# Fourier stage of a two-layer FNet and multi-query kernel: y tiles as 64-row matmuls in the score banks, a block's layer norm by VectorE, query weights split two steps ahead, and other times for the early maxima

## The chip, the cores and the metric

The kernel runs on one core of one Trainium2 chip. The metric is device time in microseconds (us), the median of repeated runs. The engines are named as in the profile: PE is TensorE's matmul (PEld its weight load), DVE is VectorE, ACT is ScalarE, POOL is GpSimd, SP is SyncE, which issues most DMAs. Each engine runs its own queue in program order. The kernel writes that order out by hand: the schedule is manual, and an instruction stands on its engine's queue where the code called it.

## The reference, cut to what matters

Two layers, each a Fourier mixing (A) and a multi-query attention (B), on 2048 rows of 512 numbers, all in float32:

```python
def _A_ref(x, dft_seq_re, dft_seq_im, dft_hid_re, dft_hid_im):
    a = jnp.einsum("bsd,ed->bse", x, dft_hid_re)
    b = jnp.einsum("bsd,ed->bse", x, dft_hid_im)
    return jnp.einsum("ts,bse->bte", dft_seq_re, a) - jnp.einsum("ts,bse->bte", dft_seq_im, b)

def _B_ref(x, wq, wk, wv, wo):            # 32 query heads of 16, one key and value head
    q = (x @ wq) ...; k = x @ wk; v = x @ wv
    p = _softmax(einsum(q, k) * 16 ** -0.5)
    return (p @ v) ... @ wo

x = A_x
for _ in range(2):
    x = x + _A_ref(_layernorm(x), ...)
    x = x + _B_ref(_layernorm(x), ...)
```

## The kernel before

A float32 product is made of three fp32r matmuls: both factors are split into a high part (a cast) and a low part (what is left), and `mm3` adds high by high, high by low, low by high. So every product below is three matmuls per 128 rows of contraction, and each operand needs a split: a cast on ACT, a subtraction on DVE or POOL.

Phase A of a layer (`phase_a`) makes the Fourier mixing, the keys and values, the queries, and some of the row maxima that the softmax needs. The 2048 output rows go in four blocks, `tb` 0 to 3, of 512. A block has 32 z steps: step `n` of phase A (0 to 127) belongs to block `n // 32`, to the cosine (c = 0) or sine (c = 1) half, and to one of 16 tiles of 128 input rows. In a step the matrix tile `craw` (loaded by SP six steps ahead, `c_load`, and split two steps ahead by ACT and POOL, `c_split`) is multiplied with the normalised input `xnh`, `xnl`: twelve matmuls of 128 rows by 512 columns. The sum over 16 steps, z, stands in four PSUM banks, two tiles of two banks named `x` (`pair()`, of which there are two; in phase B they hold the scores). After 16 steps `evac` splits z into `zh`, `zl`.

After a block's 32 steps, `y_tile` makes the block's four output tiles: 24 matmuls each of z with the hidden matrix (`dh`, `dl`), in a bank named `y` (three of them), then DVE adds the residual, POOL stores the tile, DVE takes the layer norm's sums (`ln_stats`). Block 3 is made apart, in the tail.

Then, among the first twelve z steps of the next block, run the block's tasks (`prep_tasks`, called "prep" below): the inverse deviation (`ln_rstd`), the layer norm (`ln_apply`), transposes (`tr`, into the one bank `z`), keys and values (`kv`, `v_tr`), and for four groups of heads the split of the query weights (`wq_load`, `wq_split`), the queries (`q_mm`) and their store to DRAM (`q_store`). Tasks stand in a dictionary by step, and run behind that step's matmuls.

`z_rows` makes two steps at a time with matmuls of 64 rows of contraction instead of 128: the upper and the lower 64 rows write two different banks, and in a second phase (`ph`) the other two. Between the two phases ACT copies two numbers of the bank to `junk`, which orders the writes of the two halves into one bank. `by_rows(n)` says from which step on: before, n >= 48, that is from the second half of block 1.

The maxima: for a query tile `i`, a key block `kb` and a pair of heads, `max_pair` makes two matmuls of 64 rows (one per row half) into two `y` banks, and DVE reduces each to its row maximum. Most are made in phase B, beside the scores, but 16 entries `(i, kb)` of the table `EARLY`, of 16 head pairs each, are made in phase A. An entry is (i, kb, slot of its queries, step of their load, start, end): its 16 pairs are spread evenly from start to end, on a scale in which a block takes 40 units, 32 for its z steps and 8 for its y tiles (each of the 32 groups of three matmuls of a block's y is a quarter of a unit). `hook` puts them into `inner`, and `within` calls them between the matmuls.

## Time and profile before

| | |
|---|---|
| median of 3 runs | 3801.16 us (3798.8 to 3802.88) |
| the profiled execution, its own time | 3804.91 us |
| its span, first to last instruction | 3803.1 us |
| busy: PE, PEld | 3675.1 us (97%), 1903.4 us (50%) |
| busy: DVE, ACT, POOL | 2793.1 us (73%), 2389.6 us (63%), 826.6 us (22%) |
| mean granted TensorE clock | 0.987 |
| phase A of the two layers, from its first matmul to the first scores | about 10 to 730 us, and 1905 to 2620 us |

Busy times of PE are those of pipelined matmuls, whose recorded spans overlap, so a busy PE still may issue slowly; the distance from one start to the next tells more. A merged row of the timeline that ends in "x2" holds two instructions. The clock column of a stretch is the mean share of full speed that was granted. A wait is put down to the work that ended last before it.

### The profile page before, as it was taken

How to read it: one execution, taken by the hardware profiler on the slowest of the kernel's cores; microseconds unless marked ns; L12 is line 12 of the kernel's file. 1: busy time of each engine (PE TensorE's matmuls, PEld its weight loads, DVE VectorE, ACT ScalarE, POOL GpSimd, SP SyncE). 2: the span in 40 equal slices, each digit the busy share in tenths (PEclk: the TensorE clock that was granted, in tenths of full speed). 3: DMA queues.
4: the chain of work that ended last, by engine and by line, in shares of the span. 5: the costliest groups of instructions: out<-in, count | busy, mean ns of one | idle time of the engine just before them, and what ended most of it. 6: DMA issues, size and time to landing. Idle time of an engine off the chain costs nothing. (4 is left out here: it accounts for less than half of the span.)

```text
span 3803.1 us, 61730 instructions
## 1 busy us (share of the span) xinstructions
PE 3675.1 (97%) x24130; PEld 1903.4 (50%) x24130; DVE 2793.1 (73%) x4743; ACT 2389.6 (63%) x3028; POOL 826.6 (22%) x1008
## 2 busy tenths in 40 slices
PE   8998989999999999999999989899999999999999
PEld 6776657633333333333377666575334333333433
DVE  5175867688888888888311758686888888888882
ACT  3222212488888888888933222225888888888888
POOL 5634333111111111111155342331000000000000
PEclk9999999999999999999999999899999999999999
DMA  5533323311111100110144332233111111001100
GB/s 181 128 131 88 110 72 102 102 32 33 49 35 32 46 21 24 33 49 23 38 133 116 112 100 84 86 92 98 32 46 35 33 33 49 23 22 46 35 22 26
DMA packets 204726, 242.84 MB, mean 64 GB/s; under 512 B 36880, under 2 KB 160784, under 8 KB 197264
## 3 DMA queue, kind: packets, MB, share of 16 engines
q1 hardware_dynamic: 199504, 222.08, 19.6%
q0 software_dynamic: 4864, 16.78, 1.6%
q8 instruction: 189, 3.10, 0.3%
q14 instruction: 105, 0.86, 0.1%
q10 hardware_dynamic: 64, 0.02, 0.0%
HBM read 174.58 MB, written 63.17 MB: 63 GB/s over the span
## 5 line engine op out<-in xcount | busy, mean ns | idle before, releaser
L745 ACT ACTIVATE slot<-x 128x1024 f32<-128x1024 f32 x1990 | 1943.1, 1027 | 334.4 <-PE x L742 271.4
L351 DVE TENSOR_REDUCE mxp<-y 128x1 f32<-128x512 f32 x3040 | 1908.3, 684 | 280.7 <-PE y L350 238.2
L756 PE MATMUL z<-slot,v 128*32 128x512 f32 x8192 | 1096.2, 605 | 1.9 <-ACT row L759 1.9
L742 PE MATMUL x<-slot,kz 64*128 64x512 f32 x2956 | 900.6, 447 | 3.7 <-DMA slot<-mt 3.6
L742 PEld LDWEIGHTS x<-slot,kz 64*128 64x128 f32 x2956 | 375.0, 185 | 731.7 <-ACT slot L745 598.5
L350 PE MATMUL y<-kz,slot 64*128 64x512 f32 x2208 | 726.2, 436 | 4.5 <-ACT mt L381 0.7
L338 DVE TENSOR_REDUCE mxe<-y 128x1 f32<-128x512 f32 x832 | 517.4, 683 | 163.3 <-PE y L336 146.7
L629 PE MATMUL x<-ch,xnh 64*128 64x512 f32 (+1 forms) x1536 | 429.4, 383 | 7.4 <-DVE slot L74 5.6
L796 POOL TENSOR_TENSOR row<-row,row 128x256 f32<-128x256 f32 x63 | 46.2, 733 | 1681.8 <-DMA row<-rd 1179.7
L629 PE MATMUL x<-ch,xnl 64*128 64x512 f32 (+1 forms) x1536 | 399.0, 359 | 0.0
L629 PE MATMUL x<-cl,xnh 64*128 64x512 f32 (+1 forms) x1536 | 398.7, 359 | 0.0
L350 PEld LDWEIGHTS y<-kz,slot 64*128 64x128 f32 x2208 | 349.6, 185 | 94.1 <-DVE mxp L351 27.4
L336 PE MATMUL y<-kz,slot 64*128 64x512 f32 (+1 forms) x1088 | 376.7, 431 | 17.5 <-DVE mxe L338 6.4
L78 POOL TENSOR_TENSOR cl<-craw,ch 128x512 fp32r<-128x512 f32 x236 | 304.8, 1306 | 260.1 <-ACT ch L77 191.7
L756 PEld LDWEIGHTS z<-slot,v 128*32 128x32 f32 x8192 | 163.5, 108 | 277.4 <-issue 249.2
L633 ACT COPY junk<-x 128x2 f32<-128x2 f32 x192 | 30.6, 159 | 390.0 <-PE x L629 296.1
L77 ACT CAST ch<-craw 128x512 fp32r<-128x512 f32 x256 | 154.5, 619 | 172.9 <-PE x L88 75.3
L629 PEld LDWEIGHTS x<-cl,xnh 64*128 64x128 f32 x1536 | 252.1, 190 | 20.5
L629 PEld LDWEIGHTS x<-ch,xnl 64*128 64x128 f32 x1536 | 251.1, 189 | 22.0
L629 PEld LDWEIGHTS x<-ch,xnh 64*128 64x128 f32 x1536 | 236.5, 189 | 35.8 <-issue 11.5
L336 PEld LDWEIGHTS y<-kz,slot 64*128 64x128 f32 x1088 | 180.8, 187 | 146.8 <-DVE mxe L338 90.2
L86 PE MATMUL y<-slot,slot 128*128 128x512 f32 x480 | 208.0, 433 | 17.4 <-ACT slot L77 7.7
(143 smaller groups left out, 3668.7 us busy)
## 6 DMA issues: line engine op xcount, KB each, us to landing
craw<-ct_in SPq DMA_DIRECT2D x112, 512.0 KB
slot<-qd SPq DMA_DIRECT2D x44, 1024.0 KB
qd<-row SPq DMA_DIRECT2D x144, 128.0 KB
od<-row SPq DMA_DIRECT2D x252, 64.0 KB
row<-x_in SPq DMA_DIRECT2D x32, 256.0 KB
mid<-row POOLq DMA_DIRECT2D x32, 256.0 KB, 2.3
craw<-ct_in SPq DMA_DIRECT2D x32, 256.0 KB
row<-mid SPq DMA_DIRECT2D x32, 256.0 KB
```

The lines of the kernel that those rows point to most:

```text
L77: nc.scalar.copy(hi, raw)
L78: (eng or nc.vector).tensor_sub(lo, raw, f(hi))
L86: nc.tensor.matmul(ps_, ah, bh, start=start, stop=False)
L336: nc.tensor.matmul(pm[g], o.qT[i][gs, pr, :], kz[gs, c0:c0 + n], start=True, stop=True)
L338: nc.vector.reduce_max(to[:, g:g + 1], pm[g], axis=AX.X)
L350: nc.tensor.matmul(pm, o.qT[i][gs, pr, :], kz[gs, kb * 512:kb * 512 + 512], start=True, stop=True)
L351: nc.vector.reduce_max(partial(i)[:, pr, g, kb:kb + 1], pm, axis=AX.X)
L629: nc.tensor.matmul(z[d][:, cols], w, hl[j][t == 1][rs_], start=m == 0 and ph == 0 and j == t == 0, stop=j == 1 and t == 2 and (ph == 0 or ...
L742: nc.tensor.matmul(st["e"][:, g, :], kz[64 * g:64 * g + KR, c * P:(c + 1) * P], o.qT[i][64 * g:64 * g + KR, cp:cp + 4, :], start=True, sto ...
L745: nc.scalar.activation(ptiles[i, s_][:, 2 * w:2 * w + 2, :], st.pop("e"), AF.Exp, scale=DH ** -0.5)
L756: nc.tensor.matmul(a[32 * j:32 * j + 32, :], v1[:, c, :], pt[:, j, :], start=c == 0, stop=c == NT - 1)
L796: nc.gpsimd.tensor_mul(bt["ot"][:, cs], bt["ot"][:, cs], bt["den"][:, cs])
```

## The change

It has five parts.

1. `y_rows` makes the y of blocks 0 to 2 (block 3 keeps `y_tile`): all four output tiles at once, as 64-row matmuls in two `pair()` tiles, the banks of z. The first phase adds, for each row half, its half of the contraction to one of the two tiles of a pair, the second phase swaps them, with the `junk` copy of ACT between. The two tiles of the first pair are added, stored and summed after 84 of the 96 pairs of matmuls, those of the second pair at the end. `within` is called after every third pair of matmuls.
2. `by_rows` holds from step 16 on, no longer from 48 on.
3. In prep, DVE applies the layer norm (`apply`), two tiles a step, where POOL applied one a step.
4. The tasks of prep are spread otherwise. In `z_rows` the tasks of the even step run in the middle of the pair of steps (`mid_tasks`), ahead of the second `junk` copy, where they ran at its end. The weights of query groups 0 and 1 are loaded at prep step 2 (before: all at step 4) and split at step 5, those of groups 2 and 3 loaded at step 4 and split right behind `q_mm(0)` and `q_mm(1)`, two steps ahead of their use (before: one). `kv` goes from step 5 to 6, `v_tr` from 6 to 7; `q_store` stands ahead of the next `q_mm`, no longer behind it.
5. `EARLY` has other times for the same 16 entries, and two of them change places.

```diff
 EARLY = [
-    (2, 0, 2, 44, 56, 63), (3, 0, 3, 45, 63, 70), (0, 0, 8, 47, 70, 78), (1, 0, 9, 50, 78, 86),
+    (2, 0, 2, 44, 55, 63), (3, 0, 3, 45, 63, 71), (0, 0, 8, 47, 71, 79.5), (1, 0, 9, 50, 79.5, 88),
...
+        def y_rows(tb, zh, zl, x1, between):
+            yp = [pair(), pair()]
+            at = 0
+            for ph in range(2):
+                for cc in range(2):
+                    for a in range(2):
+                        for kk, k in enumerate((0, 2, 1, 3)):
+                            for t in range(3):
+                                for r in range(2):
+                                    j = (r + ph) % 2
+                                    rs_ = slice(64 * r, 64 * r + 64)
+                                    ts_ = slice((2 * a + j) * P, (2 * a + j + 1) * P)
+                                    w = (zl if t == 2 else zh)[cc][rs_, k, ts_]
+                                    nc.tensor.matmul(yp[a][:, j, :], w, (dl if t == 1 else dh)[cc][rs_, k, :],
+                                                     start=ph == cc == kk == t == 0, stop=cc == 1 and kk == 3 and t == 2,
+                                                     skip_group_check=True)
+                            between(at)
+                            at += 1
+                        if cc == 1 and ph == 0:
+                            nc.scalar.copy(junk, yp[a][:, :, 0])
+                        elif cc == 1:
+                            for j in range(2):
+                                nc.vector.tensor_add(x1[2 * a + j], yp[a][:, j, :], x1[2 * a + j])
+                                nc.gpsimd.dma_start(mid[4 * tb + 2 * a + j], x1[2 * a + j])
+                            for j in range(2):
+                                ln_stats(x1[2 * a + j], 4 * tb + 2 * a + j)
...
-            ts[0] = [alloc, lambda: ln_apply(x1[0], x1[0], 4 * tb, nc.gpsimd)]
-            for j in range(1, 4):
-                ts[j] = [lambda j=j: ln_apply(x1[j], x1[j], 4 * tb + j, nc.gpsimd), lambda j=j: tr(j - 1)]
-            ts[4] = [lambda: tr(3)]
-            ts[4] += [lambda: [wq_load(g) for g in range(4)]]
-            ts[5] = [do_kv, lambda: wq_split(0)]
-            ts[6] = [lambda: v_tr(4 * tb, 4, st["vt"])]
+            def apply(*tts):
+                for tt in tts:
+                    ln_apply(x1[tt], x1[tt], 4 * tb + tt)
+
+            ts[0] = [alloc, lambda: apply(0, 1)]
+            ts[1] = [lambda: apply(2, 3), lambda: tr(0)]
+            ts[2] = [lambda: tr(1), lambda: wq_load(0), lambda: wq_load(1)]
+            ts[3] = [lambda: tr(2)]
+            ts[4] = [lambda: tr(3), lambda: wq_load(2), lambda: wq_load(3)]
+            ts[5] = [lambda: wq_split(0), lambda: wq_split(1)]
+            ts[6] = [do_kv]
+            ts[7] = [lambda: v_tr(4 * tb, 4, st["vt"])]
+            ts[8] = []
             for g in range(4):
-                ts[7 + g] = [lambda g=g: q_mm(tb, g, *st["xt"])]
-                if g:
-                    ts[7 + g].append(lambda g=g: q_store(tb, g - 1))
-                if g < 3:
-                    ts[7 + g].append(lambda g=g: wq_split(g + 1))
-            ts[11] = [lambda: q_store(tb, 3)]
+                ts[7 + g].append(lambda g=g: q_mm(tb, g, *st["xt"]))
+                if g < 2:
+                    ts[7 + g].append(lambda g=g: wq_split(g + 2))
+                ts[8 + g] = [lambda g=g: q_store(tb, g)]
...
             def by_rows(n):
-                return n >= 48
+                return n >= 16
...
-            def z_rows(n, ops, m, cols, c):
+            def z_rows(n, ops, m, cols, c, mid_tasks=lambda: None):
...
                             within((n, 4 * ph + 2 * dd + j))
+                            if ph == 0 and dd == j == 1:
+                                mid_tasks()
                         if ph == 0:
                             nc.scalar.copy(junk, zp[dd][:, :, cols.start])
...
-                    z_rows(n - 1, [(s - 1, hl), (s, hl)], s // 2, slice(0, 512), c)
-                    for fn in tasks.pop(n - 1, ()):
-                        fn()
+                    z_rows(n - 1, [(s - 1, hl), (s, hl)], s // 2, slice(0, 512), c,
+                           lambda: [fn() for fn in tasks.pop(n - 1, ())])
...
                 if n % 32 == 31 and tb < 3:
-                    for tt in range(4):
-                        y_tile(tb, tt, zh, zl, x1[tt], {k: inner.pop(("y", tb, 8 * tt + k), ()) for k in range(8)})
+                    y_rows(tb, zh, zl, x1, lambda k: within(("y", tb, k)))
```

What moves, at three places. On PE, in the y of block 1 of the first layer (`slot_278` to `slot_281` are the hidden matrix, the other slots z's parts and, beside `kz`, the queries; L86 to L88 are `mm3`, L336 a pair of maxima); before:

```order
L86 MATMUL y<-slot_278,slot_1592 128x512
L87 MATMUL y<-slot_279,slot_1592 128x512
L88 MATMUL y<-slot_278,slot_1593 128x512
L336 MATMUL y<-kz,slot_1618 128x512 x2
L86 MATMUL y<-slot_278,slot_1592 128x512
L87 MATMUL y<-slot_279,slot_1592 128x512
L88 MATMUL y<-slot_278,slot_1593 128x512
```

Now (L401 is `y_rows`; "x2" are the two row halves, and the maxima's two are row halves too):

```order
L401 MATMUL x<-slot_278,slot_2067 128x512 x2
L336 MATMUL y<-kz,slot_2143 128x512 x2
L401 MATMUL x<-slot_278,slot_2066 128x512 x2
L401 MATMUL x<-slot_279,slot_2066 128x512 x2
L401 MATMUL x<-slot_278,slot_2067 128x512 x2
```

Before, a pair of 64-row maxima stood between matmuls of 128 rows; now all in this stretch have 64 rows.

On DVE, at the end of the same y and the first steps of prep (`row` are the output tiles, L338 the maxima's reduction); before, the last tile's add and sums, and all that follows up to the maxima in the fourth prep step:

```order
L398 TENSOR_TENSOR row_2075<-y,row_2075 128x512
L135 BN_STATS bst<-row_2075 128x6
L136 BN_AGGR mv<-bst 128x2
L338 TENSOR_REDUCE mxe<-y 128x1 x8
L157 TENSOR_SCALAR lnv<-mv 128x4
L161 RECIPROCAL rs<-lnw 128x4
L173 TENSOR_TENSOR lnw<-rs 128x4
L174 TENSOR_TENSOR lnw<-lnw,lnv 128x4
L176 TENSOR_SCALAR lnw<-lnw 128x4
L178 TENSOR_TENSOR rs<-rs,lnw 128x4
L338 TENSOR_REDUCE mxe<-y 128x1 x16
```

Now, from the second pair's adds on:

```order
L410 TENSOR_TENSOR row_2579<-x,row_2579 128x512
L410 TENSOR_TENSOR row_2581<-x,row_2581 128x512
L135 BN_STATS bst<-row_2579 128x6
L136 BN_AGGR mv<-bst 128x2
L135 BN_STATS bst<-row_2581 128x6
L136 BN_AGGR mv<-bst 128x2
L338 TENSOR_REDUCE mxe<-y 128x1 x4
L157 TENSOR_SCALAR lnv<-mv 128x4
L161 RECIPROCAL rs<-lnw 128x4
```

The adds and sums of two tiles now stand in one lump (the first pair's lump stands two reductions ahead of these rows), the reductions between it and `lnv` are four, not eight, and behind `rs` follow `row_2575<-row_2575,mv,rs` and three more of L182, which POOL had.

On ACT, in the first pair of prep steps of block 1, now (L666 is `junk` of `z_rows`, L159 the square root of `ln_rstd`, L81 and L82 the split behind a transpose):

```order
L666 COPY junk<-x 128x2
L159 ACTIVATE lnw<-lnv 128x4
L666 COPY junk<-x 128x2
L81 ACTIVATE row_5319<-z 128x512
L82 CAST slot_5276<-row_5319 128x4x128
```

Before (L633 is `junk`, L159 the square root):

```order
L633 COPY junk<-x 128x2 x2
L159 ACTIVATE lnw<-lnv 128x4
L81 ACTIVATE row_4687<-z 128x512
L82 CAST slot_4681<-row_4687 128x4x128
L77 CAST ch<-craw 128x512 x2
```

Both copies of `junk` stood ahead of the square root; now it stands between them.

6 rows, old and new, of the table EARLY are left out of this document.

## The prediction

> **What bounds the kernel now.** I read the page first, then the stretches of phase A in the view by windows, then the timeline where a stretch takes longer than its matmuls.
>
> ```profile
> span 3803.1 us, 61730 instructions
> PE 33%; DVE 1%; ACT 0%; DMA 0%; issue 0%; SPq 0%; ACTq 0%; DVEq 0%
> ```
>
> The chain that ended last runs through PE wherever it names an engine. So time is won where PE's starts lie further apart than they must. The change touches phase A alone; phase B keeps the same maxima to make, since `EARLY` holds the same 16 entries. The stretches below are, in order: y of block 0, prep of block 0, steps 46 to 63, y of block 1, its prep (steps 64 to 75), steps 76 to 95, y of block 2, its prep (96 to 107), 108 to 117, 118 to 127, and steps 48 to 129 of the first and of the second layer.
>
> ```profile
> core 0: us, PE busy (x) PEld busy (x) DVE busy (x) ACT busy (x) POOL busy (x), PEclk, DMA share, GB/s
> 107.78:129.89 22.11, 22.09 (x97) 17.94 (x96) 4.71 (x9) 4.13 (x8) 6.83 (x7) 1.00 0.10 36
> 129.89:189.07 59.18, 51.45 (x225) 39.57 (x224) 5.00 (x11) 19.83 (x36) 43.66 (x40) 1.00 0.62 133
> 194.65:257.47 62.82, 60.53 (x482) 47.27 (x480) 46.44 (x74) 17.74 (x42) 25.12 (x21) 1.00 0.50 177
> 257.47:291.59 34.12, 34.12 (x130) 20.26 (x130) 24.68 (x42) 4.31 (x8) 6.57 (x7) 1.00 0.15 54
> 291.59:374.25 82.66, 70.75 (x433) 50.64 (x432) 43.17 (x74) 19.16 (x44) 38.00 (x28) 0.90 0.29 77
> 374.25:453.55 79.30, 77.95 (x599) 54.30 (x599) 72.71 (x119) 21.98 (x52) 30.64 (x24) 1.00 0.43 137
> 453.55:497.84 44.29, 42.02 (x143) 22.69 (x144) 33.56 (x55) 3.48 (x6) 5.55 (x7) 1.00 0.16 61
> 497.84:588.28 90.44, 77.39 (x451) 50.73 (x447) 53.87 (x93) 19.06 (x44) 37.93 (x28) 0.91 0.27 72
> 588.28:634.81 46.53, 44.46 (x453) 35.64 (x454) 41.42 (x69) 13.07 (x35) 17.92 (x14) 0.96 0.41 131
> 634.81:700.61 65.80, 63.25 (x655) 55.39 (x651) 41.21 (x81) 13.91 (x45) 17.48 (x23) 1.00 0.14 47
> 201.61:710.13 508.52, 472.88 (x3369) 340.33 (x3370) 360.66 (x612) 114.68 (x282) 179.56 (x152) 0.96 0.30 94
> 2092.10:2600.98 508.88, 473.20 (x3369) 340.02 (x3369) 360.69 (x612) 114.70 (x282) 179.52 (x152) 0.96 0.30 92
> ```
>
> The first row gives PE's unit: 96 matmuls of 128 by 512 in 22.11 us, 0.23 us each. The two layers' stretches are alike (508.5 and 508.9 us), so I work one layer and double.
>
> What maxima cost between matmuls of 128 rows, and what 64-row pairs cost among themselves:
>
> ```profile
> 258.04 0.40 PE L88 MATMUL y<-slot,slot 128*128 128x512 f32 x1
> 258.36 0.49 PE L336 MATMUL y<-kz,slot 64*128 64x512 f32 x2
> 258.79 0.50 PE L86 MATMUL y<-slot,slot 128*128 128x512 f32 x1
> 259.12 0.39 PE L87 MATMUL y<-slot,slot 128*128 128x512 f32 x1
> ...
> 296.24 0.61 PE L629 MATMUL x<-cl,xnh 64*128 64x512 f32 x2
> 296.47 0.61 PE L629 MATMUL x<-ch,xnl 64*128 64x512 f32 x2
> ```
>
> From L88 to L87 three steps take 1.08 us where three units are 0.69: a round trip from 128 rows to 64 and back costs 0.39 us. Two 64-row matmuls on different halves share one unit (296.24 to 296.47).
>
> The Trainium skill speaks against cutting a matmul in two: "TensorEngine Tiling (Array Packing)", section "Instruction Overhead", gives each matmul about 60 cycles of overhead on this chip. The change issues 1344 more (576 in six y, 768 in the z of steps 16 to 47); at the 2.4 GHz of "TensorE: Matmul & The Clock Gate" that would by estimate be 34 us. The rows above show none of it, since the pair takes 0.23 us as the single does, so the sum goes without it.
>
> Then the waits of prep:
>
> ```profile
> 299.07 0.16 DVE L157 TENSOR_SCALAR lnv<-mv 128x4 f32<-128x4 f32 x1
> 300.31 0.16 DVE L178 TENSOR_TENSOR rs<-rs,lnw 128x4 f32<-128x4 f32 x1
> 300.58 4.13 POOL L182 TENSOR_SCALAR row<-row,mv,rs 128x512 f32<-128x512 f32 x2 [4.48 <-DVE rs L178]
> 302.70 1.12 PE L251 MATMUL z<-ident,row 128*128 128x128 f32 x4 [3.99 <-POOL row L182]
> 306.05 0.63 PE L629 MATMUL x<-cl,xnh 64*128 64x512 f32 x2
> 306.47 0.63 PE L629 MATMUL x<-ch,xnl 64*128 64x512 f32 x2
> ...
> 323.07 0.49 PE L86 MATMUL y<-slot,wkvh 128*128 128x512 f32 x1 [1.40 <-ACT slot L82]
> ...
> 325.45 0.63 PE L87 MATMUL y<-slot,wkvh 128*128 128x512 f32 x1
> 325.87 0.63 PE L88 MATMUL y<-slot,wkvl 128*128 128x512 f32 x1
> ...
> PE z L251 <- POOL row L182: 24.8, 10, 4.8
> PE y L88 <- POOL slot L78: 10.0, 10, 1.4
> PE y L86 <- ACT slot L77: 7.7, 4, 1.9
> ```
>
> PE stood 3.99 us for the layer norm, and then issued at 0.42 us instead of 0.23; it did so again at 325, behind a wait of 1.40. The clock column says why: 0.90 and 0.91 in the two preps is (1 - 0.90) x 2 x 82.66 = 16.5 us at half clock in the first and 16.3 in the second, each worth up to 8 us. The last two rows are the query weights, split too late.
>
> The Trainium skill ("TensorE: Matmul & The Clock Gate", section "What's actually happening") lets the clock fall only after an idle window of about 3.4 us. By that rule all the half-clock time goes once no wait is so long; that is the second case below.
>
> **The sum.** Prices of DVE and ACT:
>
> ```profile
> 440.48 3.68 DVE L338 TENSOR_REDUCE mxe<-y 128x1 f32<-128x512 f32 x6 [0.24 <-PE x L629]
> 463.97 0.68 DVE L398 TENSOR_TENSOR row<-y,row 128x512 f32<-128x512 f32 x1
> 465.51 2.54 DVE L338 TENSOR_REDUCE mxe<-y 128x1 f32<-128x512 f32 x4
> L182 DVE TENSOR_SCALAR row<-row,mv,rs 128x512 f32<-128x512 f32 x24 | 21.4, 894 | 4.5 <-POOL rs L151 4.3
> 355.08 0.60 ACT L81 ACTIVATE row<-y 128x512 f32<-128x512 f32 x1 [7.39 <-PE y L88]
> 355.71 0.62 ACT L82 CAST row<-row 128x512 fp32r<-128x512 f32 x1
> 356.24 0.61 ACT L77 CAST slot<-row 128x512 fp32r<-128x512 f32 x1
> ```
>
> A pair of maxima costs DVE 3.68 / 3 = 1.23 us, a tile's add and sums 1.54 (463.97 to 465.51), the inverse deviation 1.4 (299.07 to 300.47), a tile's layer norm 0.89.
>
> *y of block 1.* Before, 112 units are 25.8 us, 16 round trips 6.2, 2 remain for banks. After, 96 + 15 units are 25.5. New: y takes the banks of z and waits for `evac`. ACT frees the first pair after a copy, a cast, a copy (1.82 us), of which 1.4 (six units) pass beside z. With its handing on 0.7, and 0.5 for reductions that come late. 26.7 for 34.1: -7.4.
>
> *Prep of block 1.* Units: 144 of z, 31 of maxima, 64 of tasks, 239, 55.0 us. Seven stays at 128 rows instead of five cost 2.7. The tasks in mid-pair put ACT work ahead of the second `junk`, for which PE waits; five of them (two transposes, `kv`, two `q_mm`) put 1.2 to 1.9 us there where PE has 1.4 us of matmuls left: 0.5 each, 0.9 for the one with a weights' cast behind it, 2.9. The layer norm: from the first lump on DVE has 3.1 + 1.2 + 3.1 + 2.5 = 9.9 us ahead of `lnv`, then root and `junk` 0.7, and PE gets there after 2.8 + 2.8 + 1.4 + 0.9 = 7.9: it waits 2.7, and 1.8 more for score maxima's banks behind four applications of 0.89. That lump moves the wait more than it removes it. `kv` and the weights have two or three steps and are hidden by z. Of the half clock I keep half, 4 us, since the row at 325 ran slow behind a wait of only 1.40 us; and 0.8 for issue. 69.9 for 82.7: -12.8.
>
> *y of block 2.* Before: 119 units are 27.4, 23 round trips 9.0, and DVE idled a quarter of it. After, PE needs 28 us, DVE 23 x 1.23 + 2 x 1.54 = 31.4 (the second pair's lump comes later); with a wait at the start and at the first lump I take 35: -9.3.
>
> *Prep of block 2.* In its first six steps DVE sets the pace: 21 x 1.23 + 3.1 + 1.4 + 3.6 = 33.9 us against 25 of PE. In the last six, 155 units are 35.7, with three stays 1.2, ACT 2.0, and a second of waiting. Half of the half clock, 4: 77.8 for 90.4: -12.6.
>
> *Steps 76 to 95.* 59 pairs of maxima become 52. Before, DVE was the bound (59 x 1.23 + 1.4 = 74 of 79.3; 1.4 are two subtractions of `evac`, priced like the add's 0.68). After, DVE needs 65.4 and PE 292 x 0.23 = 67.2 and one hand-over of banks, 0.60 + 0.62 and the handing on, 68.6; so near each other I add 3.4: 72.0, -7.3.
>
> *The rest.* 108 to 117 lose three pairs, -3.7. 118 to 127 get nine more: between 9 x 0.23 = 2.1 and 9 x 1.23 = 11.1, I take +6, since DVE is busy 41 of 66 us but not at the same steps. 46 to 63: two units fewer, -0.5. Block 0 has no maxima, so its prep now pays stays at 128 rows (2.7) and ACT (2.9), and loses its waits of 11.3 (59.18 less 208 units): with 1.3 for the lump and 0.7 at y's start, 55.5, and I take -3. Steps 16 to 47 as 64-row pairs: `z_rows` ran 4.8 us over its units in 194.65 to 257.47, with two hand-overs in it; over sixteen pairs between 0 and 8, nearest the clean rows at 0.23: +1.5.
>
> Queues passed: SP now takes two weight loads two steps earlier, where they wait for the transposes of the rows that they overwrite, at most a step; the matrix tiles behind them are wanted four steps on, which covers it. Gone, that cover would cost each block one z step, 2.8 us. POOL loses four times 2.07 us a block and gets nothing. Six stores a group go ahead of a `q_mm` and wait for POOL's subtraction of the step before, as they did.
>
> Sum per layer: -7.4 - 12.8 - 9.3 - 12.6 - 7.3 - 3.7 + 6 - 0.5 - 3 + 1.5 = -49.1; twice, -98. From the profiled execution's 3804.9 us: **3707 us**. That execution is 3.7 us above the median of the runs, inside this sum's roughness. A difference under 0.2% could not be told from none.
>
> **The rivals.**
>
> *More than that (chance 0.20).* No wait is long enough for the clock to fall (-8 a layer), y of block 2 keeps PE's pace (-6.5), the tail hides its nine pairs (-4): 37 us more, 3670. For it: PE's units are only 28 of 35 us there. Against: half clock behind the wait of 1.40 us.
>
> *Less (0.13).* DVE in its order is the true bound: the lumps and denser maxima give back what the round trips freed. y of block 2 then gains 4, its prep 4, steps 76 to 95 gain 3, the tail pays 11.1: 23 a layer less, 3753. For it: DVE is busy 72.7 of 79.3 us in 374 to 453. Against: over the whole 508.5 us it is busy 361.
>
> *Each matmul has its overhead (0.04).* If 64-row pairs lose 25 ns for the extra matmul once the weights change each time, 1344 of them add 34 us: 3741. The 0.23 us of the rows above stands against it.
>
> *Slower (0.05).* ACT runs in order, and six mid-pair chains a block (root, two transposes, `kv`, two `q_mm`) now stand ahead of a `junk` for which PE waits, 36 in all. It decides from 98 / 36 = 2.7 us each over what is counted; at 3.3, a root that waits for all reductions ahead of it, 3826. Against: only the root waits for DVE, the others are 1.2 to 1.9 us long.
>
> **How the numbers follow.** The likeliest case has 0.58, within 3680 to 3740. The range 3664 to 3760 holds it, the larger gain and most of the smaller one, and leaves out the slower case and the ends. Faster by over 0.2%: 0.94; within: 0.02; slower: 0.04 (a part of the slower case only comes to nothing).
>
> **What would show it.** The y of block 1 near 27 us with maxima's matmuls 0.23 us after their neighbours; the y of block 2 near 35, DVE nearly full; the preps near 70 and 78 with a clock of 0.95; no waits of L251 for POOL and of L86, L88 for the weights, but new ones of `z_rows` for `junk` behind L159. Wrong would be: y as long as before, the clock still at 0.90, or waits for `junk` of 3 us in every step of prep.

## The result, and the profile after

The changed kernel takes 3716.76 us (median of 4 runs, 3712.24 to 3724.12) against 3800.56 us (4 runs, 3798.8 to 3802.88) for the kernel before in the same session: a ratio of 0.9781, 95% interval 0.9764 to 0.9798. The forecast was 3707 us with a range of 3664 to 3760. The profiled execution took 3724.12 us, 7.4 over that median, and its span is 80.8 us less than that of before. One execution, the profiled one of the run with `junk` first below, took 3973.3 us at a granted clock of 0.829; it is left out of that run's median, and no stage is read from its trace.

The page of the changed kernel:

```profile
PE 3631.1 (98%) x25474; PEld 1909.3 (51%) x25474; DVE 2798.4 (75%) x4767; ACT 2400.3 (64%) x3104; POOL 777.3 (21%) x984
PE 41%; DVE 3%; ACT 1%; DMA 0%; issue 0%; SPq 0%; POOL 0%; DVEq 0%; ACTq 0%
```

PE's busy time fell by 44 us only, though 1344 more matmuls ran: it is still the engine on which the chain runs, but DVE's share of that chain rose from 1% to 3%. The view by windows, stage by stage in the first layer, with the columns of the prediction (prep of block 0; steps 44 to 47; 48 to 63; y of block 1; prep 64 to 75; 76 to 95; y of block 2; 96 to 101; 102 to 107; 108 to 117; 118 to 127; and 48 to 129 as a whole):

```profile
133.91:189.21 55.30, 54.13 (x371) 38.76 (x368) 9.09 (x20) 20.39 (x47) 37.28 (x38) 1.00 0.62 155
189.21:206.92 17.71, 14.09 (x103) 10.75 (x100) 2.13 (x4) 4.35 (x11) 7.38 (x7) 0.84 0.96 319
206.92:260.67 53.75, 53.03 (x450) 46.46 (x448) 42.48 (x67) 15.65 (x39) 22.26 (x18) 0.99 0.36 121
260.67:286.18 25.51, 25.51 (x222) 20.95 (x224) 19.92 (x32) 4.41 (x9) 5.24 (x5) 1.00 0.11 42
286.18:355.70 69.52, 67.63 (x431) 47.25 (x427) 46.16 (x84) 20.64 (x47) 32.65 (x28) 0.95 0.41 107
355.70:429.86 74.16, 72.82 (x586) 54.03 (x587) 66.99 (x108) 19.86 (x49) 28.25 (x23) 1.00 0.44 142
429.86:462.87 33.01, 30.65 (x240) 22.61 (x241) 30.56 (x52) 4.40 (x9) 5.75 (x6) 0.97 0.14 49
462.87:497.53 34.66, 31.95 (x205) 20.30 (x202) 30.58 (x58) 9.29 (x22) 15.40 (x14) 0.93 0.37 122
497.53:543.39 45.86, 44.09 (x256) 28.95 (x255) 29.34 (x49) 11.25 (x25) 16.71 (x14) 1.00 0.40 95
543.39:588.63 45.24, 43.17 (x447) 35.06 (x449) 39.55 (x66) 11.65 (x32) 16.17 (x13) 0.96 0.38 115
588.63:660.81 72.18, 68.28 (x672) 58.11 (x669) 51.77 (x99) 14.14 (x45) 17.50 (x23) 1.00 0.13 43
206.92:670.33 463.41, 445.29 (x3559) 341.46 (x3557) 361.69 (x618) 115.59 (x286) 163.46 (x143) 0.98 0.32 98
```

Two stretches of before that the prediction showed only inside longer ones (steps 44 to 47; 102 to 107), in the same view:

```profile
189.07:201.61 12.54, 11.32 (x50) 8.86 (x48) 0.69 (x1) 3.58 (x6) 8.72 (x9) 1.00 0.92 240
542.44:588.28 45.84, 41.76 (x238) 27.71 (x237) 25.85 (x42) 11.06 (x25) 16.42 (x13) 0.91 0.33 75
```

The last row of the changed kernel stands against 508.52 us: from step 48 on a layer gains 45.1 us (second layer 45.3). Ahead of step 48 it loses: steps 14 to 47 take 6.6 us more in the first layer and 4.0 more in the second. That makes 80 of the 80.8 us. The gain lies where the change is (y 25.5 and 33.0 for 34.1 and 44.3, prep of block 1 69.5 for 82.7); steps 102 to 107 gained nothing (45.86 for 45.84, with 23 pairs of maxima for 20), although their clock rose from 0.91 to 1.00.

How the y of block 1 reads now, on PE's timeline:

```profile
260.67 0.96 PE L401 MATMUL x<-slot,slot 64*128 64x512 f32 x6 [0.20 <-ACT row L81]
261.47 0.39 PE L336 MATMUL y<-kz,slot 64*128 64x512 f32 x2
261.70 1.55 PE L401 MATMUL x<-slot,slot 64*128 64x512 f32 x12
263.09 0.40 PE L336 MATMUL y<-kz,slot 64*128 64x512 f32 x2
```

A pair of maxima starts at 261.47 and its successor at 261.70, one unit of 0.23 us; before, such a place cost 0.62. The twelve matmuls behind it take 1.39 us, six units. The wait for z's banks is 0.20.

What the forecast had not seen are two waits for a DMA ahead of step 48. The first is at step 47, PE's timeline:

```profile
202.06 0.80 PE L336 MATMUL y<-kz,slot 64*128 64x512 f32 x2 [3.62 <-DMA slot<-qd]
202.65 0.63 PE L660 MATMUL x<-ch,xnh 64*128 64x512 f32 x2
203.08 0.63 PE L660 MATMUL x<-cl,xnh 64*128 64x512 f32 x2
```

and the load's issue, on SP's queue:

```profile
194.66 0.83 SPq L359 DMA_DIRECT2D slot<-qd  x2
```

The first early maxima now start at 55 on the table's scale, a step before 48. The load of their queries is a task of step 44, which begins at 189.21, but SP has it behind a dozen stores of the queries and the load of a matrix tile, and issues it at 194.66, in steps in which the DMA engines are full (share 0.96, 319 GB/s). PE goes on 7.4 us after that issue. It stands 3.62 us and then issues every 0.43 us instead of 0.23, that is at about half clock. The second is at step 20 of the first layer, on ACT and PE:

```profile
79.19 0.62 ACT L77 CAST wkvh<-row 128x512 fp32r<-128x512 f32 x1 [4.49 <-DMA row<-wkv_in]
80.44 0.50 PE L660 MATMUL x<-ch,xnh 64*128 64x512 f32 x2 [3.19 <-ACT junk L666]
```

The cast of the key and value weights is a task of step 20 and waits for their load. Since tasks now run in mid-pair, it stands ahead of `junk`, and PE waits for `junk`: steps 20 to 25 take 21.8 us instead of 16.8, once.

### The profile page after: what moved, and what is told of

It reads as the page before. It is cut to its first block, busy times and chain, and to the rows that moved or that the text cites. A ratio compares the mean times of both kernels' runs of the same rounds, so it can differ in the third digit from the quotient of the medians.

```text
span 3722.3 us, 64512 instructions
## 1 busy us (share of the span) xinstructions
PE 3631.1 (98%) x25474; PEld 1909.3 (51%) x25474; DVE 2798.4 (75%) x4767; ACT 2400.3 (64%) x3104; POOL 777.3 (21%) x984
## 5 line engine op out<-in xcount | busy, mean ns | idle before, releaser
L338 DVE TENSOR_REDUCE mxe<-y 128x1 f32<-128x512 f32 x832 | 516.4, 682 | 189.4 <-PE y L336 184.7
L660 PE MATMUL x<-ch,xnh 64*128 64x512 f32 (+1 forms) x2048 | 507.8, 390 | 16.3 <-DVE slot L74 8.9
L660 PE MATMUL x<-ch,xnl 64*128 64x512 f32 (+1 forms) x2048 | 475.2, 369 | 0.0
L660 PE MATMUL x<-cl,xnh 64*128 64x512 f32 (+1 forms) x2048 | 474.7, 369 | 0.0
L350 PEld LDWEIGHTS y<-kz,slot 64*128 64x128 f32 x2208 | 349.5, 185 | 94.5 <-DVE mxp L351 27.5
L336 PE MATMUL y<-kz,slot 64*128 64x512 f32 (+1 forms) x1088 | 354.3, 420 | 33.7 <-DVE mxe L338 20.7
L660 PEld LDWEIGHTS x<-ch,xnh 64*128 64x128 f32 x2048 | 268.7, 189 | 69.2 <-issue 16.4
L660 PEld LDWEIGHTS x<-ch,xnl 64*128 64x128 f32 x2048 | 280.7, 189 | 33.3
L660 PEld LDWEIGHTS x<-cl,xnh 64*128 64x128 f32 x2048 | 281.7, 190 | 28.0
L666 ACT COPY junk<-x 128x2 f32<-128x2 f32 x256 | 40.5, 158 | 332.3 <-PE x L660 253.6
L336 PEld LDWEIGHTS y<-kz,slot 64*128 64x128 f32 x1088 | 171.8, 188 | 129.4 <-DVE mxe L338 90.5
L338 DVE TENSOR_REDUCE mxp<-y 128x1 f32<-128x512 f32 (+1 forms) x256 | 144.4, 617 | 24.7 <-PE y L336 21.5
```

The lines of the kernel that those rows point to most:

```text
L336: nc.tensor.matmul(pm[g], o.qT[i][gs, pr, :], kz[gs, c0:c0 + n], start=True, stop=True)
L338: nc.vector.reduce_max(to[:, g:g + 1], pm[g], axis=AX.X)
L350: nc.tensor.matmul(pm, o.qT[i][gs, pr, :], kz[gs, kb * 512:kb * 512 + 512], start=True, stop=True)
L660: nc.tensor.matmul(z[d][:, cols], w, hl[j][t == 1][rs_], start=m == 0 and ph == 0 and j == t == 0, stop=j == 1 and t == 2 and (ph == 0 or ...
L666: nc.scalar.copy(junk, zp[dd][:, :, cols.start])
```

## The experiments

Each is an edit of the changed kernel unless it says otherwise, and each was timed beside the kernel before; the changed kernel's own ratio is 0.9781 (0.9764 to 0.9798). Rows are from the first layer, by windows.

**Part 1 undone: y as matmuls of 128 rows.**

```diff
-                    y_rows(tb, zh, zl, x1, lambda k: within(("y", tb, k)))
+                    for tt in range(4):
+                        y_tile(tb, tt, zh, zl, x1[tt], {k: inner.pop(("y", tb, 8 * tt + k), ()) for k in range(8)})
```

> The changed kernel with one part undone: the y of blocks 0 to 2 again as 128-row matmuls in the y banks, with the maxima's 64-row pairs between. Theory (the round trips between 128 and 64 rows are what the y stretches saved): y of block 1 goes from 25.9 to about 33.5 us and y of block 2 from 33.4 to about 43, two layers, less 2 us a block in the preps whose VectorE lump is spread again: total about 3747 (3738 to 3757) against 3717. Rival (VectorE's reductions set the pace of block 2's y whatever PE's rows are): y of block 2 grows by under 3 us, total under 3735.

Measured: 3746.05 us (3745.49 to 3750.28), ratio 0.9854 (0.9837 to 0.987). The y of blocks 1 and 2:

```profile
259.86:294.00 34.14, 32.58 (x128) 19.79 (x126) 23.82 (x41) 4.33 (x8) 6.58 (x7) 1.00 0.15 54
433.85:477.58 43.73, 42.13 (x143) 22.90 (x144) 33.15 (x55) 3.98 (x7) 6.16 (x7) 1.00 0.12 43
```

The two y are back at the times of before, 8.6 and 10.7 us more, while the prep behind the first gets 3.9 us shorter (65.65 for 69.52; 1.4 in the second layer) and steps 96 to 101 get 2.9 shorter in both. So part 1 is worth some 28 us, by the two ratios, and a part of what it gains comes back as longer preps. The run does not part two causes: y lost its round trips, and it also left the `y` banks to the maxima. By the prediction's rows, 16 round trips of 0.39 us are 6.2 of the 8.6 us.

**Part 1 alone, put into the kernel before.**

```diff
-                    for tt in range(4):
-                        y_tile(tb, tt, zh, zl, x1[tt], {k: inner.pop(("y", tb, 8 * tt + k), ()) for k in range(8)})
+                    y_rows(tb, zh, zl, x1, lambda k: within(("y", tb, k)))
```

> The kernel before with one part of the change alone: the y tiles as pairs of 64-row matmuls in the score banks. Theory: y of block 1 falls from 34.1 to about 26 us and y of block 2 from 44.3 to 33 or 34 us, the steps behind each give 2 to 4 us back, since the maxima that VectorE did during y and the layer norm now stand closer together; a layer gains (8.5 + 10.5 - 5) us, and the kernel takes 3772 us (3765 to 3780). Rival: without the other times of the maxima and with the layer norm still on POOL, the wait behind y gives all of it back, and the kernel takes over 3790 us.

Measured: 3775.87 us (3774.59 to 3777.36), ratio 0.9934 (0.992 to 0.9949). The y of block 1, and the prep behind it:

```profile
258.74:286.14 27.40, 25.85 (x224) 21.04 (x226) 22.42 (x38) 4.40 (x9) 5.77 (x6) 1.00 0.16 59
286.14:368.07 81.93, 68.93 (x434) 48.33 (x430) 44.67 (x78) 19.16 (x44) 38.50 (x29) 0.94 0.30 81
```

The time is inside the theory's range, by terms that differ from it: y of block 1 gains 6.7 and not 8.5, that of block 2 10.7, the prep behind it gives nothing back (81.93 us for 82.66), steps 96 to 101 give back 2.8 (47.40 for 44.60). So part 1 gains 25 of the 84 us alone, and some 28 among the others. This run also shows what parts 2 to 5 are worth together: without them the prep of block 1 takes 81.93 us, with them 69.52.

**Part 2 undone: 64-row z from step 48 on, as before.**

```diff
-                return n >= 16
+                return n >= 48
```

> The changed kernel with z as 64-row pairs only from step 48 on, as before; block 0's prep then runs beside 128-row z, its tasks behind every step. Theory (part 2 buys nothing where there are no maxima and costs stays at 128 rows and ScalarE chains): steps 32 to 43 fall from 55.3 to about 51 us in each layer, and the wait at step 20 goes (5 us once): total about 3704 (3699 to 3709). Rival (the finer hooks of the 64-row pairs are what sped up block 0's prep from 59.2): steps 32 to 43 return to 57 to 59, total 3716 to 3722.

Measured: 3702.43 us (3700.8 to 3707.53), ratio 0.9738 (0.9723 to 0.9752). The prep of block 0:

```profile
129.74:180.50 50.76, 50.19 (x227) 40.14 (x225) 8.75 (x20) 19.84 (x36) 35.96 (x37) 1.00 0.72 164
```

50.76 us for 55.30, and the same in the second layer (50.88 for 55.41): part 2 costs 4.5 us a layer there, the mid-pair tasks of block 0 included, which only `z_rows` has. Steps 20 to 25 are back at 16.7 us, since no `junk` stands there any more. Twice 4.5 and 5.0 make the 14 us.

**Part 3, its engine undone: POOL applies the layer norm,** two tiles a step as DVE did, not one as before.

```diff
-                    ln_apply(x1[tt], x1[tt], 4 * tb + tt)
+                    ln_apply(x1[tt], x1[tt], 4 * tb + tt, nc.gpsimd)
```

> The changed kernel with the layer norm of a block applied by GpSimd again, at the new places. Theory (it was the place in the order that PE waited for, not the engine; VectorE's queue now sets the pace of prep): steps 96 to 107 fall from 80.5 to 77.5 to 79 us, 64 to 75 from 69.5 to 68 to 69.5, no waits of the transposes above 1 us, total 3707 to 3715. Rival (GpSimd at 2.07 us a tile was the wait): the transposes wait 2 to 4 us in each block again, total 3727 to 3740.

Measured: 3727.64 us (3723.92 to 3730.86), ratio 0.9802 (0.9787 to 0.9816), which overlaps that of the changed kernel. The prep of block 1:

```profile
289.58:358.48 68.90, 66.12 (x431) 46.33 (x428) 44.33 (x80) 20.62 (x47) 40.66 (x32) 0.98 0.41 108
```

DVE's layer norm is worth 2.9 us where DVE has nothing else to do (block 0, 58.18 for 55.30). In block 1, where the maxima keep DVE busy, POOL does as well (68.90 for 69.52), and in block 2 better (78.57 for 80.52). So the layer norm's engine alone is not where the 13 us of the prep come from. The two profiled executions differ by 1.0 us (spans of 3723.3 and 3722.3), so their stages do not show the 11 us between the medians.

**Part 4, its order on ACT: tasks in mid-pair, but behind `junk`.**

```diff
-                            if ph == 0 and dd == j == 1:
-                                mid_tasks()
                         if ph == 0:
                             nc.scalar.copy(junk, zp[dd][:, :, cols.start])
+                            if dd == 1:
+                                mid_tasks()
```

> The changed kernel with one order turned: in the middle of a pair of steps the second junk copy stands ahead of the tasks, not behind them; PE's order is the same. Theory (ScalarE's order holds PE: the root behind VectorE's queue and, once, a cast behind a DMA, stand ahead of the copy): steps 64 to 75 fall from 69.5 to about 66.5 us, 96 to 107 from 80.5 to 78.5, 32 to 43 from 55.3 to 54, and the one wait at step 20 of the first layer (4.97 us over its units) goes: total about 3700 (3695 to 3706). Rival (the wait only moves to the maxima's banks, since VectorE is what is behind): 64 to 75 and 96 to 107 change by under 1 us, only step 20 gains, total 3709 to 3714.

Measured: 3715.22 us, ratio 0.9767 (0.975 to 0.9783). That cannot be told from the changed kernel and is not the theory's 3700 us: the chains that stand ahead of `junk` on ACT cost nothing that shows, or no more than the one wait at step 20 (5.0 us).

**Part 4, its place: tasks at the pair's end.**

```diff
-                    z_rows(n - 1, [(s - 1, hl), (s, hl)], s // 2, slice(0, 512), c,
-                           lambda: [fn() for fn in tasks.pop(n - 1, ())])
+                    z_rows(n - 1, [(s - 1, hl), (s, hl)], s // 2, slice(0, 512), c)
+                    for fn in tasks.pop(n - 1, ()):
+                        fn()
```

> The changed kernel with the tasks of prep's even steps at the end of the pair again, as before the change. Theory (half a pair of steps between the layer norm and the transposes, and between two groups of queries, is what the mid-pair place bought): steps 32 to 43 go from 55.3 to about 58, 64 to 75 from 69.5 to about 74, 96 to 107 from 80.5 to about 84, and step 20 of the first layer loses its 5 us wait: total 3728 to 3738. Rival (ScalarE's chains ahead of the second junk copy cost as much as the place bought): preps within 1 us of what they were, total 3708 to 3716.

Measured: 3727.1 us (3725.88 to 3727.94), ratio 0.9803 (0.9789 to 0.9816), whose interval just overlaps that of the changed kernel. Prep of block 1:

```profile
286.76:361.03 74.27, 67.61 (x434) 47.13 (x430) 47.81 (x86) 18.99 (x44) 30.90 (x26) 0.95 0.35 96
```

Mid-pair tasks are worth 4.7 us in block 1 (2.5 in the second layer) and 1.6 at steps 96 to 101 (0.4), and nothing in block 0 (55.80 for 55.30) or in 102 to 107, which are 1.7 us shorter here. Steps 20 to 25 lose 3.2 of their 5 us.

**Part 4, the query weights: split one step ahead again.**

```diff
-            ts[5] = [lambda: wq_split(0), lambda: wq_split(1)]
+            ts[5] = [lambda: wq_split(0)]
...
-                if g < 2:
-                    ts[7 + g].append(lambda g=g: wq_split(g + 2))
+                if g < 3:
+                    ts[7 + g].append(lambda g=g: wq_split(g + 1))
```

> The changed kernel with the query weights split one step ahead again, as before the change (wq_split of group g+1 in step 7+g, one split in step 5). Theory: each split (ACT cast of 0.62 us, POOL subtraction of 1.3 us, and their places in the engines' queues) ends just too late for the next step's query matmuls, so the steps that carry them (72-75, 102-107 and 38-43) lose 1 to 2 us a block, some 3 to 5 us a layer, and the kernel takes 3726 us (3722 to 3730). Rival: half a step's z matmuls (above 2.8 us) cover the split, no stretch moves by more than 2 us in a layer in sum, and the time stays at 3714 to 3719 us.

Measured: 3726.51 us (3724.03 to 3729.36), ratio 0.9806 (0.979 to 0.9823). The prep of block 1:

```profile
289.36:358.35 68.99, 64.81 (x432) 45.22 (x428) 46.06 (x84) 20.52 (x47) 32.60 (x28) 1.00 0.41 108
```

The total is the theory's and the stages are nearly the rival's: 1.5 us a layer in block 0 (56.77 for 55.30), nothing in block 1 and 0.1 in steps 102 to 107, where the maxima between the matmuls probably give the split its time. The profiled span, 3722.8 us, equals that of the changed kernel, and the two ratios' intervals overlap: the stages alone show a cost, 3 us for both layers.

**Part 5 undone: the table of before** (one entry starts a unit later, because its keys do).

```diff
-    (2, 0, 2, 44, 55, 63), (3, 0, 3, 45, 63, 71), (0, 0, 8, 47, 71, 79.5), (1, 0, 9, 50, 79.5, 88),
-    (2, 1, 0, 65, 88, 92), (0, 1, 8, None, 92, 98), (1, 1, 9, None, 98, 104.5), (4, 0, 2, 79, 104.5, 110.5),
+    (2, 0, 2, 44, 56, 63), (3, 0, 3, 45, 63, 70), (0, 0, 8, 47, 70, 78), (1, 0, 9, 50, 78, 86),
+    (2, 1, 0, 65, 87, 91), (0, 1, 8, None, 91, 96.5), (1, 1, 9, None, 96.5, 102), (4, 0, 2, 79, 102, 107.5),
...
```

> The changed kernel with the table of before (part 5 undone), but for one entry of block 1's keys that starts one unit later, at 87, since its keys are now made a step later. Theory: part 5 is worth nothing or less. Undone, steps 76 to 95 get 7 pairs back and lose 5 us, steps 108 to 117 get 3 back and lose 2, but 118 to 127 lose 9 pairs and gain 6 us at the 0.7 us that a pair cost there, 102 to 107 lose 3 pairs and gain 2, and the wait for the query tile at step 47 goes, 5 us: some 6 us a layer less, 3705 us (3699 to 3711). Rival, by the terms of the prediction: part 5 gains 7.3 in steps 76 to 95 and 3.7 in 108 to 117 and pays 6 in 118 to 127, so that undoing it costs 5 us a layer, 3727 us (3721 to 3733).

Measured: 3716.69 us (3716.24 to 3720.32), ratio 0.9781 (0.9765 to 0.9797). Steps 76 to 95:

```profile
357.53:436.20 78.67, 77.42 (x602) 54.06 (x598) 73.09 (x120) 20.04 (x49) 28.72 (x23) 1.00 0.41 135
```

Stage by stage much as the theory said (-5.1 in steps 44 to 47, which take 12.64 us, +4.5 in 76 to 95, -6.4 in 118 to 127 and -2.0 in 102 to 107; the y of block 1 and steps 48 to 63 pay 1.9 and 2.3, which it had not), but the median is the changed kernel's to 0.1 us, where the theory had 12 less and the rival 10 more. Part 5 is worth nothing that shows: what the new table saves in steps 76 to 95, 48 to 63 and the y of block 1, it pays in 118 to 127, in 102 to 107 and at step 47.

**The two DMA waits taken away.**

```diff
-    (2, 0, 2, 44, 55, 63), ...
+    (2, 0, 2, 44, 56, 63), ...
...
-        split_sb(r, wkvh, wkvl)
+        wkv_raw.append(r)
+    def split_wkv():
+        split_sb(wkv_raw.pop(), wkvh, wkvl)
...
-                add(20, load_wkv)
+                add(17, load_wkv)
+                add(21, split_wkv)
```

> The changed kernel with two waits for transfers taken away: the first early entry starts at 56 again, not at 55 (one z step more for its queries to land), and the key and value weights are loaded at step 17 and split at step 21, not both at step 20. Theory (3.6 us of PE's wait and 2.3 us at half clock behind it, in each layer at step 47; 5 us at steps 20 to 25 of the first): steps 44 to 47 fall from 17.7 to about 13 us in both layers, steps 20 to 25 of the first layer from 21.8 to 16.8, total about 3702 (3696 to 3708). Rival (the transfer lands later than one step; the wait moves to step 48): steps 44 to 63 together fall by under 2 us a layer, total 3708 to 3714.

Measured: 3710.09 us (3706.9 to 3710.6), ratio 0.9757 (0.9743 to 0.977). Steps 20 to 25 and 44 to 47:

```profile
74.53:91.33 16.80, 16.80 (x147) 13.49 (x144) 4.57 (x6) 8.01 (x19) 10.59 (x12) 1.00 0.82 229
185.96:198.56 12.60, 11.32 (x98) 8.85 (x95) 0.69 (x1) 4.36 (x11) 7.34 (x7) 1.00 0.97 294
```

Both waits are gone, 5.0 us once and 5.1 and 4.8 in the two layers, while steps 48 to 63 pay 1.2 and 0.9. The median gains 6.7 where 13 would follow from the profiles, of which that of the changed kernel stands 7.4 us over its median; the two ratios' intervals overlap. The size of the wait at step 47 varies: in the profiles of six kernels here that keep this wait and differ elsewhere, steps 44 to 47 take 15 to 20 us.

**Fewer maxima at the keys of block 2: 18 pairs in steps 102 to 107 for 23, 36 in 108 to 117 for 31.**

```diff
-    ..., (4, 1, 0, 96, 126, 130),
+    ..., (4, 1, 0, 96, 126, 135),
```

> The changed kernel with one entry of the early maxima spread over more steps: (4, 1) from 126 to 135, not to 130, which takes 6 of 23 pairs out of steps 102 to 107 and puts them into 108 to 111. Theory (steps 102 to 107 are bound by VectorE locally: eight pairs in three stretches of z of about 3.7 us of PE's units need 4.9 us of VectorE each, and the query matmuls between hold no maxima): steps 102 to 107 fall from 45.9 to 40 to 42 us, by more than the 1.4 us of six units; 108 to 117 rise by 4 to 7; total within 3 us. Rival (PE's and ScalarE's chains set these steps): they fall by 1.4 to 2 us only.

Measured: 3722.0 us (3719.43 to 3733.11), ratio 0.9795 (0.9781 to 0.9809). Steps 102 to 107 and 108 to 117:

```profile
493.42:536.47 43.05, 41.77 (x246) 28.06 (x246) 23.65 (x39) 11.25 (x25) 17.48 (x14) 1.00 0.46 114
536.47:586.32 49.85, 46.54 (x458) 35.61 (x459) 45.47 (x76) 11.65 (x32) 15.42 (x12) 1.00 0.30 93
```

Five pairs fewer save 2.8 us, 0.56 each, which lies between the theory (4 to 6) and the rival (1.4 to 2); five more cost 4.6, 0.92 each. In neither place is a pair as cheap as PE's 0.23.

**The pieces that paid, or cost nothing in the stretches they were meant for, together:** part 2 undone, both DMA waits away, POOL's layer norm for blocks 1 and 2, tasks behind `junk`.

> The changed kernel with what the first runs point to: z as 64-row pairs from step 48 on only, the first entry at 56, the key and value weights' split not behind their load, the layer norm by GpSimd in the blocks with maxima and by VectorE in block 0, and the second junk copy ahead of the mid-pair tasks. By the stretches of the single runs: -4.5 a layer and -5 once for block 0, -4.5 a layer at step 47, -2.5 a layer for the layer norm, 0 to -2 a layer for the order of the copy: -28 to -32 from 3717, total about 3688 (3680 to 3696). If the gains overlap (the wait at 47 half gone already in the run from step 48 on): 3693 to 3699.

Measured: 3697.22 us (3696.08 to 3697.31), ratio 0.9724 (0.9711 to 0.9737): better than both kernels, and with runs that agree to 1.2 us where those of the changed kernel spread over 12. It is the case in which the gains overlap, and its interval overlaps that of the run with part 2 undone alone (3702.43 us), so the other pieces are not shown to add to it.

**On top of that, a table that puts pairs where they cost 0.23:** against the version just shown, 8 pairs more in steps 48 to 63, 6 more in the y of block 1, 11 fewer in its prep.

```diff
-    (2, 0, 2, 44, 56, 63), (3, 0, 3, 45, 63, 71), (0, 0, 8, 47, 71, 79.5), (1, 0, 9, 50, 79.5, 88),
-    (2, 1, 0, 65, 88, 92), (0, 1, 8, None, 92, 98), ...
+    (2, 0, 2, 44, 56, 62.4), (3, 0, 3, 45, 62.4, 68.6), (0, 0, 8, 47, 68.6, 74.6), (1, 0, 9, 50, 74.6, 80.4),
+    (2, 1, 0, 65, 87, 91), (0, 1, 8, None, 91, 97), ...
```

> The best version so far (3697 us: 64-row x matmuls from step 48 on only, first early entry from 56 on, key and value weights loaded in step 17 and split in step 21, junk first, POOL for the layer norm of block 0) with a table that moves pairs of maxima out of the steps where a pair cost 0.65 to 1.15 us into those where it cost its 0.23 us on TensorE alone (the end of 48-62, 76-95), and none beside the layer norm of block 1. Theory: 4 to 6.5 us a layer less, 3685 us (3681 to 3691). Rival: the stretches that take the pairs (48-62, y of block 1, 76-95) become bound by VectorE at 1.2 us a pair and give it back; the kernel takes 3694 us or more.

Measured: 3714.06 us (3712.39 to 3716.79), ratio 0.9772 (0.9758 to 0.9787): 17 us slower than without. Steps 48 to 63, y of block 1 and its prep, first of the version above, then of this one:

```profile
194.13:249.16 55.03, 53.78 (x453) 44.45 (x453) 43.84 (x69) 15.64 (x39) 22.20 (x19) 1.00 0.47 173
249.16:274.46 25.30, 25.30 (x222) 22.34 (x224) 19.75 (x32) 4.40 (x9) 5.23 (x5) 1.00 0.11 43
274.46:343.47 69.01, 66.26 (x431) 46.31 (x428) 44.26 (x80) 21.14 (x47) 40.68 (x32) 0.98 0.41 108
```

```profile
194.11:252.82 58.71, 57.90 (x468) 43.47 (x468) 51.51 (x83) 15.63 (x39) 22.23 (x19) 1.00 0.44 165
252.82:284.28 31.46, 29.11 (x236) 21.42 (x237) 29.14 (x50) 4.40 (x9) 5.77 (x6) 1.00 0.14 51
284.28:352.19 67.91, 63.44 (x410) 44.47 (x408) 29.75 (x54) 21.05 (x47) 39.68 (x30) 0.97 0.38 101
```

The rival held. With 21 pairs DVE is busy 29.1 of 31.5 us in the y of block 1, and the six pairs cost 6.2 us there. The prep they left lost a third of DVE's work (44.3 to 29.8 us) and got 1.1 us shorter.

## Why the prediction was right, and where its steps were off

The mechanism was the forecast one, and its case the likeliest: 3717 for 3707. The gain was put too high, 98 us against 80.8 between the two profiles, and it came this near partly by luck, since the terms missed to both sides. By its terms, in us per layer, first and second layer, from the same stretches of the two profiles:

| term | forecast | measured |
|---|---|---|
| y of block 1 | -7.4 | -8.6, -8.7 |
| prep of block 1 | -12.8 | -13.1, -13.9 |
| steps 76 to 95 | -7.3 | -5.2, -5.2 |
| y of block 2 | -9.3 | -11.3, -11.3 |
| prep of block 2 | -12.6 | -9.9, -10.3 |
| steps 108 to 117 | -3.7 | -1.3, -1.3 |
| steps 118 to 127 | +6 | +6.4, +7.3 |
| steps 44 to 63 | -0.5 | +3.1, +3.1 |
| y and prep of block 0 | -3 | -4.1, -1.8 |
| 64-row z, measured from 14 to 31 | +1.5 | +5.5, +0.6 |

- **Round trips.** Right in kind and a little small. Pairs in y cost 0.23 us, and undoing part 1 brings back both y. The y of block 2 is DVE's: busy 30.6 of 33.0 us, with the work as counted; the two waits added to it were too much. Of the case "less", in which this y gained 4 us, nothing came there (11.3); steps 76 to 95 went half its way. On the rule of the Trainium skill ("TensorEngine Tiling (Array Packing)", section "Instruction Overhead") that each matmul has some 60 cycles of overhead, the y of block 0 decides: 21.93 us now with 192 matmuls, 22.11 before with 96. Steps 20 to 25 say the same of z: 16.80 us in the run without the DMA waits and 16.80 before, with twice the matmuls. Nothing of the estimated 34 us came.
- **Prep of block 1.** The sum was right, its parts were not. The wait for the layer norm was forecast as 2.7 and 1.8 us, and half the half clock was kept as 4. DVE's timeline shows the lump as it was counted:

```profile
284.61 1.28 DVE L410 TENSOR_TENSOR row<-x,row 128x512 f32<-128x512 f32 x2
...
293.76 0.16 DVE L157 TENSOR_SCALAR lnv<-mv 128x4 f32<-128x4 f32 x1
```

  From the first add to `lnv` 9.2 us pass, where 9.9 were counted. But PE did not stand for it. It ran at half clock meanwhile: (1 - 0.95) x 2 x 69.52 is 7 us, worth 3.5. The second layer's prep, the same instructions in the same execution, shows a clock of 0.98 and takes 68.85; in the run with the weights split one step ahead the clock is 1.00 and the time 68.99. So the half clock cost some half a microsecond here, probably because PE would have waited for DVE otherwise. Wait and clock were priced as two terms and were nearly one. What lies above the units is mostly DVE's: the weight loads of the maxima wait 6.1 us in all for its reductions.
- **Half clock behind short waits.** PE's timeline in the same place:

```profile
288.13 0.50 PE L336 MATMUL y<-kz,slot 64*128 64x512 f32 x1 [0.85 <-DVE mxe L338]
...
289.92 0.79 PE L660 MATMUL x<-ch,xnh 64*128 64x512 f32 x2 [0.61 <-DVE row L410]
290.51 0.63 PE L660 MATMUL x<-cl,xnh 64*128 64x512 f32 x2
290.94 0.63 PE L660 MATMUL x<-ch,xnl 64*128 64x512 f32 x2
```

  PE issues at 0.43 us behind two waits of under a microsecond. The Trainium skill ("TensorE: Matmul & The Clock Gate", section "What's actually happening") has the clock fall after an idle window of about 3.4 us. Here no such window preceded, so the measurement decides, and against the case "more than that", of which it was one leg.
- **Prep of block 2.** Its first six steps were counted by DVE, 33.9 us, and took 34.7. The last six were counted by PE's units, its stays, ACT and a second of waiting, 39.9 us, and took 45.9 at a clock of 1.00. By luck the sum stayed near: the half clock, counted as 4 us on top, did not show there, and the first six steps ran at 0.93 and yet took only 0.8 us more than DVE's count. In the last six PE waits for DVE as well, whose queue runs in order:

```profile
507.46 1.39 DVE L269 TENSOR_TENSOR kz<-y,kz 16x512 fp32r<-16x512 f32 x2 [3.42 <-ACT kz L266]
508.89 4.88 DVE L338 TENSOR_REDUCE mxe<-y 128x1 f32<-128x512 f32 x8
```

  DVE stands 3.42 us for ACT's part of the keys, with eight reductions behind it that PE then waits for. The weight loads of the maxima wait 7.4 us in all for the reductions in these six steps.
- **Steps 76 to 95 and 108 to 117.** Both mis-sized by about 2 us: the pairs taken out were priced at or near DVE's 1.23 (7.3 / 7 and 3.7 / 3), and went at 0.74 (5.2 / 7) and 0.43 (1.3 / 3). Steps 118 to 127 paid 0.71 a pair (6.4 / 9), as taken.
- **Steps 44 to 63: the step that failed.** It was costed by its two units, and the start of the first entry, a step earlier, was not followed to the load it waits for: 5.2 us a layer, with its half clock, against 2.1 gained behind it. Where the sum had -0.5, a layer paid 3.1. The row of before for steps 44 to 47, with the DMA engines at 0.92, is the one that should have been read.
- **Steps 16 to 31.** The rival "slower" was there, at step 20: a chain on ACT that waits for a DMA ahead of `junk`, 5.0 us once. Elsewhere it was not. PE's waits, in total, times and longest:

```profile
PE y L336 <- DVE mxe L338: 20.7, 19, 2.4
PE x L660 <- ACT junk L666: 5.3, 5, 3.2
```

  Five waits for `junk` in two layers, one of them the 3.2 at step 20; the other four, of under 0.7 us, are in block 0's preps. In those of blocks 1 and 2, where 2.9 and 2.0 us were counted for ACT, there is none. The largest sum is that for score banks behind DVE's reductions: what is left is DVE's pace.
- **Block 0.** The 5.6 us that stays at 128 rows and ACT were to cost are 4.5 with part 2 undone. The Trainium skill ("TensorEngine Tiling (Array Packing)", section "Key Properties") says that a change of tiling mode drains TensorE. The trace fits this with 0.39 us a round trip; it does not show the drain itself.

One by one the parts of the prep are worth little: POOL's layer norm and the later split each cost block 1 nothing, the table of before next to nothing (69.89 us), mid-pair tasks 2.5 to 4.7 of its 13 us. Together they are worth 12.4 (81.93 without parts 2 to 5), so they cover for each other, as far as the rest does not lie with what was not tried alone: `kv`, `v_tr` and `q_store` at their old steps, one tile of the layer norm a step. The waits for the layer norm show such cover; with part 1 alone, with DVE at the old place, with POOL at the new one:

```profile
PE z L251 <- POOL row L182: 25.5, 10, 4.8
PE z L251 <- DVE row L182: 11.9, 6, 2.6
PE z L251 <- POOL row L182: 4.1, 5, 1.5
```

The changed kernel has no such wait, the kernel before 24.8 us. The new place alone takes most of it away, the engine alone half.

## What to carry to other kernels

An added pair of maxima cost what the engine that paced its stretch took for it, so one table move has two prices: look at both ends by windows before moving work from a full stretch to an "idle" one, and count the pairs per step, not per stage. When an operation starts one step earlier, follow each operand back to its DMA and read the DMA share there. When work is moved ahead of a copy that another engine waits for, look for the one task among it that waits for a transfer.

## What the runs showed of the hardware that was not expected

A pair of 64-row maxima cost from 0.10 us (11 pairs taken from the prep of block 1: 1.1 us) over 0.46 (8 added in steps 48 to 63: 3.7 us) to 1.03 us (6 added in y of block 1: 6.2 us), while its matmuls take 0.23 at full clock. And half clock is not always lost time: by the clock column the prep of block 1 had some 7 us of it in the first layer and some 3 in the second, and took 69.52 and 68.85 us.
